# Two grouped-query decode attentions on one core: one cache's K and V loaded in 16 KB runs instead of 8 KB

## The chip, the cores and the metric

The kernel runs on one core of a Trainium2 chip. The time is the device time of one execution in microseconds (us). The profile's span is something else: it runs from the first to the last instruction that the profile records, and here it is about 1.5 us shorter than the time. The experiments were timed in three calls on three chips, so each is compared with the runs of before in its own call.

In the profile PE is the tensor engine's matmuls, PEld its weight loads, DVE the vector engine, ACT the scalar engine, POOL the general engine, and SP the engine that issues the DMAs.

## The reference, cut to what matters

The program computes two independent attention steps for a single new token, A and B, and puts their results side by side. A attends only to the last 2,048 tokens of its cache, B to all 8,192.

```python
# both: x (1,1,576), 32 query heads, 16 KV heads, head size 128, caches (1,16,8192,128), bf16
def attend(x, k_cache, v_cache, wq, wo):
    q = (x @ wq).reshape(1, 1, 32, 128)          # every KV head serves 2 query heads
    k, v = k_cache, v_cache                      # A: the last W = 2048 tokens only
    p = softmax(q @ k.T * 128 ** -0.5)
    return (p @ v).reshape(1, 1, 4096) @ wo      # (1, 1, 576)
out = concatenate([attend(A), attend(B)], axis=-1)
```

Almost no arithmetic is done on each byte that is read. A has 16 MB of K and V, B has 64 MB, the four weight matrices have 18 MB (MB and KB are binary in this paragraph and for packet sizes).

## The kernel before

K and V pass through four 32 KB-per-partition slots in on-chip memory: two for K (`s` = 0, 1), two side by side for V. A run below is a stretch of contiguous bytes that is copied as one; the trace shows one DMA packet for each (2,048 packets of 8 KB for A). The work is cut into five groups of 16 MB: group 0 is all of A, groups 1 to 4 are four heads of B each. The PE program is a loop over the groups; the other engines' programs are unrolled. All large loads go out on SP's queue (the two small x on ACT's), in the order wq of A, wq of B, then K, K, V of each group, then both wo.

```python
def load_k(g, s):                       # 4 MB into slot s
    if g:                               # B: 2 heads, 128 tokens = 32 KB a run
        i = 4 * (g - 1) + 2 * s
        return sp.dma_start(dst, ks[1][0, i:i + 2, :, :].rearrange("e (p t) d -> p e (t d)", t=128))
    for m in range(4):                  # A: 4 DMAs of 2 heads, 32 tokens = 8 KB a run
        i = 4 * m + 2 * s
        src = ks[0][0, i:i + 2, SK - W_A:, :].rearrange("e (p t) d -> p e (t d)", t=32)
        ins = sp.dma_start(dst[:, m * UNIT:(m + 1) * UNIT], src)
        ...                             # cut: semaphore bookkeeping

def load_v(g):                          # 8 MB into both V slots
    if g:                               # B: 4 heads, 256 tokens = 64 KB a run
        return sp.dma_start(dst, vs[1][0, 4 * g - 4:4 * g, :, :].rearrange("h (p t) d -> p h (t d)", t=256))
    for i in range(8):                  # A: 8 DMAs, again 8 KB a run
        m, c = divmod(i, 2)
        src = vs[0][0, 4 * m:4 * m + 4, SK - W_A:, :].rearrange("h (p c t) d -> p h c (t d)", c=2, t=32)[:, :, c, :]
        ...
```

The K tiles are transposed on PE and evicted by ACT and DVE in turn (`L501`, `L504`), then scores, softmax and V sums follow:

```python
if q % 2 == 0: act.activation(kt[:, u % NKT, q * 1024:(q + 1) * 1024], ktps_bf[q], ACT.Copy)   # L501
else:          dve.tensor_copy(kt[:, u % NKT, q * 1024:(q + 1) * 1024], ktps_bf[q])            # L504

def v_sums(g, place):                   # 64 matmuls in the PE loop, the same for every group, L572
    for c in range(2):
        for tt in range(8):
            for j in range(4):
                pe.matmul(opsum[32 * j:32 * j + 32, :], lhsT=ptm[...], rhs=v[:, c, :, b:b + 128], ...)
```

POOL zeroes tiles and makes masks by `affine_select` at the start, later copies slices of q.

```python
for t in (ident, xpad, selq, warm, identf, same, pick, qst): pool.memset(t[:], 0.0)
...
for dj in range(-3, 4): pool.affine_select(same ...)     # 7 selects, L379
for j in range(4):      pool.affine_select(pick ...)     # 4 selects, L379
```

## Time and profile before

| | before |
|---|---|
| time, median of 3 runs | 246.94 us (246.59 to 247.2) |
| profiled run: time / span | 246.54 / 245.0 us |
| data read | 102.8 MB |
| busy: PE / ACT / DVE | 66% / 37% / 34% |

The page of the kernel before, parts 1 to 3, cut. Part 2's rows are 40 equal slices of the span; DMA is the busy share of the 16 DMA engines in tenths:

```profile
span 245.0 us, 5228 instructions
PE 160.8 (66%) x2325; PEld 117.3 (48%) x2325; DVE 82.3 (34%) x145; ACT 91.1 (37%) x95; POOL 10.7 (4%) x48
...
DMA  9999999999999999899999999999989999989993
...
q1 hardware_dynamic: 5052, 102.77, 98.2%
```

No compute engine is near full, and the data queue's packets fill 98.2% of the engines' time. The same in stretches (window, length, busy time and instruction count of PE, PEld, DVE, ACT and POOL, granted PE clock, DMA share, GB/s):

```profile
26.00:56.00 30.00, 22.00 (x336) 17.68 (x324) 12.61 (x23) 15.90 (x17) 0.32 (x2) 0.83 1.01 422
104.00:143.00 39.00, 28.37 (x400) 20.78 (x400) 15.00 (x22) 17.67 (x18) 0.63 (x4) 0.85 1.00 430
143.00:182.00 39.00, 29.09 (x400) 20.75 (x400) 15.01 (x22) 17.58 (x18) 0.63 (x4) 0.81 1.00 432
```

The first line is A's K and V, the others are groups of B. Both are full, but A moves fewer bytes per microsecond. With the DMA engines at a share of 1.00 to 1.01 in these stretches, what is left to change there is the cost of a byte.

Groups by line inside A's stage (30 to 66 us): busy us and mean ns of one, then idle time ahead:

```profile
L501 ACT ACTIVATE kt<-ktps 128x1024 bf16<-128x1024 bf16 x16 | 15.7, 1021 | 13.2 <-PE ktps L495 13.2
L504 DVE COPY kt<-ktps 128x1024 bf16<-128x1024 bf16 x16 | 11.1, 692 | 15.4 <-PE ktps L495 15.4
```

The timeline: POOL's two series of selects, A's V sums, and the issue of B's first V, which A's V sums release:

```profile
3.64 2.91 POOL L379 TENSOR_SCALAR_AFFINE_SELECT same<-same 128x128 f32<-128x128 f32 x7
...
6.75 2.97 POOL L379 TENSOR_SCALAR_AFFINE_SELECT pick<-pick 128x512 f32<-128x512 f32 x4
...
65.88 5.82 PE L572 MATMUL opsum<-slots,ptm 128*32 128x512 bf16 x64 [3.54 <-PEq L214]
...
71.75 0.55 SPq L422 DMA_DIRECT2D slots<-in_B_v_cache_dram  x1
```

The end of the chain that ended last (start, us, what):

```profile
229.58 0.33 SPq L398
229.90 0.04 issue
229.95 12.34 DMA slots<-in_B_wo_dram
242.29 0.04 issue
242.33 0.64 PE ktps L665 x16
242.97 0.02 issue
242.99 0.31 DVE outsb L673
```

The last thing that arrives is a piece of B's wo; 0.64 us of matmuls, a copy, the store of the output and the closing barrier follow.

### The profile page before, as it was taken

The page shows a single profiled execution, that of the slowest core. Times are in us where ns is not written, and L with a number is a line of the kernel's source. Part 1 is how long each engine was busy: PE and PEld are TensorE (multiplying, and loading weights), DVE is VectorE, ACT ScalarE, POOL GpSimd, SP SyncE. Part 2 cuts the span into 40 slices and gives each one's busy share as a digit, 9 for nine tenths or more (in the row PEclk, how much of TensorE's full clock was granted, in tenths as well). Part 3 has the DMA queues.
Part 4 walks back from the last instruction along what each step waited for, and adds up shares of the span by engine and source line. Part 5 has one row for each costly group of instructions (what it writes and reads, how often), then busy time and mean ns, then how long its engine had stood idle before and what let it go on. Part 6 is the DMA issues. An engine that isn't in the chain of part 4 may idle for free. (4 is left out here: it accounts for less than half of the span.)

```text
span 245.0 us, 5228 instructions
## 1 busy us (share of the span) xinstructions
PE 160.8 (66%) x2325; PEld 117.3 (48%) x2325; DVE 82.3 (34%) x145; ACT 91.1 (37%) x95; POOL 10.7 (4%) x48
## 2 busy tenths in 40 slices
PE   0006329994476999383999454999456699647654
PEld 0002129782226876233887221987232678337533
DVE  0001304653222465303556312455322455442300
ACT  2000006875003786301778300687600568620000
POOL 7400000000000000000000000000000000000000
PEclk9999857999575999768899857799857999995999
DMA  9999999999999999899999999999989999989993
GB/s 337 434 434 391 424 427 415 420 423 420 464 428 428 508 397 449 375 428 428 481 419 449 401 407 433 439 492 407 471 375 428 439 482 417 449 386 409 432 402 153
DMA packets 5222, 102.89 MB, mean 420 GB/s; under 512 B 731, under 2 KB 861, under 8 KB 1117
## 3 DMA queue, kind: packets, MB, share of 16 engines
q1 hardware_dynamic: 5052, 102.77, 98.2%
q8 instruction: 6, 0.10, 0.2%
q10 hardware_dynamic: 160, 0.00, 0.0%
q14 instruction: 4, 0.02, 0.0%
HBM read 102.76 MB, written 0.00 MB: 419 GB/s over the span
## 5 line engine op out<-in xcount | busy, mean ns | idle before, releaser
L501 ACT ACTIVATE kt<-ktps 128x1024 bf16<-128x1024 bf16 x80 | 77.9, 1021 | 90.1 <-PE ktps L495 90.1
L495 PE MATMUL ktps<-ident,slots 128*128 128x128 bf16 x1280 | 85.0, 230 | 23.0 <-PEq L214 23.0
L495 PEld LDWEIGHTS ktps<-ident,slots 128*128 128x128 bf16 x1280 | 79.1, 104 | 38.3 <-issue 38.3
L504 DVE COPY kt<-ktps 128x1024 bf16<-128x1024 bf16 x80 | 55.3, 692 | 62.0 <-PE ktps L495 62.0
L572 PE MATMUL opsum<-slots,ptm 128*32 128x512 bf16 x320 | 28.2, 528 | 10.6 <-PEq L214 10.6
L516 PE MATMUL sacc<-kt,qst 128*32 128x512 bf16 x320 | 25.4, 392 | 1.9 <-PEq L214 1.9
L572 PEld LDWEIGHTS opsum<-slots,ptm 128*32 128x32 bf16 x320 | 13.7, 127 | 23.7 <-issue 21.7
L551 PE MATMUL misc<-ident,psb 128*128 128x128 bf16 x40 | 4.7, 288 | 15.8 <-PEq L214 15.8
L538 ACT ACTIVATE psb<-sacc,stat 128x2048 bf16<-128x2048 f32 x5 | 9.8, 1967 | 9.5 <-DVE stat L531 9.5
L583 DVE TENSOR_TENSOR vtmp<-opsum,maskV 128x512 f32<-128x512 f32 x4 | 2.8, 692 | 30.9 <-PE opsum L572 30.9
L551 PEld LDWEIGHTS misc<-ident,psb 128*128 128x128 bf16 x40 | 3.6, 128 | 18.2 <-issue 18.2
L438 PE MATMUL misc<-xnine,twice 64*128 64x18 bf16 x1 | 0.2, 170 | 18.0 <-DMA xnine<-in_B_x_dram 18.0
L485 POOL COPY qst<-qcol 128x8 bf16<-128x8 bf16 x20 | 3.1, 191 | 161.9 <-PE sacc L516 147.5
L665 PE MATMUL ktps<-slots,opj 128*32 128x144 bf16 (+1 forms) x192 | 6.8, 247 | 4.4 <-DMA slots<-in_B_wo_dram 4.4
L558 DVE TENSOR_TENSOR ptm<-misc,maskP 128x1024 bf16<-128x1024 bf16 x5 | 3.5, 692 | 16.0 <-PE misc L551 16.0
L516 PEld LDWEIGHTS sacc<-kt,qst 128*32 128x32 bf16 x320 | 5.0, 94 | 8.0 <-issue 4.3
L438 PEld LDWEIGHTS misc<-xnine,twice 64*128 64x128 bf16 x1 | 0.1, 98 | 18.0 <-issue 18.0
L665 PEld LDWEIGHTS ktps<-slots,opj 128*32 128x32 bf16 x192 | 5.2, 97 | 5.9 <-DMA slots<-in_B_wo_dram 5.3
L462 ACT ACTIVATE qrow<-opsum 128x512 bf16<-128x512 f32 x1 | 0.6, 597 | 19.4 <-PE opsum L456 19.4
L447 DVE TENSOR_SCALAR xpad<-misc,par 128x5 bf16<-128x5 f32 (+1 forms) x8 | 1.2, 230 | 14.2 <-PE misc L438 14.2
L529 DVE TENSOR_REDUCE stat<-sacc 128x1 f32<-128x512 f32 x5 | 3.5, 692 | 4.5 <-PE sacc L516 4.5
L551 PE MATMUL turned<-ident,psb 128*128 128x128 bf16 x40 | 4.8, 293 | 0.0
(73 smaller groups left out, 52.5 us busy)
## 6 DMA issues: line engine op xcount, KB each, us to landing
slots<-in_B_k_cache_dram SPq DMA_DIRECT2D x8, 4096.0 KB
slots<-in_A_k_cache_dram SPq DMA_DIRECT2D x8, 1024.0 KB
slots<-in_A_v_cache_dram SPq DMA_DIRECT2D x8, 1024.0 KB
slots<-in_A_wq_dram SPq DMA_DIRECT2D x1, 4608.0 KB, 13.8
slots<-in_B_wq_dram SPq DMA_DIRECT2D x1, 4608.0 KB, 23.9
slots<-in_A_wo_dram SPq DMA_DIRECT2D x1, 4608.0 KB, 20.8
slots<-in_B_wo_dram SPq DMA_DIRECT2D x1, 3024.0 KB, 27.6
slots<-in_B_wo_dram SPq DMA_DIRECT2D x1, 1008.0 KB, 11.7
```

Of the source, the lines that this page charges most:

```text
L485: ins = pool.tensor_copy(dst, src)
L495: ins = pe.matmul(ktps_bf[q][:, t * 128:(t + 1) * 128], lhsT=slots[:, o:o + 128], rhs=ident[:, :], start=True, stop=True, is_transpose=True)
L501: add("act", lambda act, q=q, dst=dst: act.activation(dst, ktps_bf[q], ACT.Copy), reads=[("bank", q)], writes=[("kt", u % NKT, q)], tag="e ...
L504: add("dve", lambda dve, q=q, dst=dst: dve.tensor_copy(dst, ktps_bf[q]), reads=[("bank", q)], writes=[("kt", u % NKT, q)], tag="e%d%d" % ( ...
L516: ins = pe.matmul(sacc[32 * j:32 * j + 32, :], lhsT=qst[:, o:o + 32], rhs=rhs, start=(u == 0 and e == 0), stop=True, skip_group_check=True)
L529: add("dve", lambda dve: dve.tensor_reduce(st(C_M + g), sacc[:, :], AX.X, ALU.max), reads=[B_S], writes=[("st", C_M + g)], tag="max")
L538: return act.activation(dst, src, ACT.Exp, bias=st(C_NB + g), scale=SCALE, accum_out=st(C_L + g))
L551: ins = pe.matmul(dst[:, t * 128:(t + 1) * 128], lhsT=psb[:, o:o + 128], rhs=ident[:, :], start=True, stop=True, is_transpose=True)
L558: return dve.tensor_tensor(ptm[:, c * 1024:(c + 1) * 1024].rearrange("p (t y) -> p t y", t=8), dst.rearrange("p (t y) -> p t y", t=8), mas ...
L572: ins = pe.matmul(opsum[32 * j:32 * j + 32, :], lhsT=ptm[:, o:o + 32], rhs=v[:, c, :, b:b + 128], start=(c == 0 and tt == 0), stop=(c == 1 ...
L583: add("dve", lambda dve: dve.tensor_tensor(vtmp[:, :, :], src, by, ALU.mult), reads=[B_O, w], writes=["vtmp"], tag="keep")
L665: ins = pe.matmul(ktps[P][32 * j:32 * j + 32, 0:w], lhsT=opj[:, P, jj:jj + 32], rhs=slots[:, o:o + w], start=(jj == 0), stop=(jj == HQ - 1))
```

## The change

The intent is to read A's K and V in runs twice as long, so in half as many packets: 64 tokens (16 KB) per partition instead of 32. That moves tokens within the tiles. K evictions of A sort them back while they write, in runs of two elements. In the V slots the head half `x` and the token half `c` change places for A, so only the matmuls with `c` equal to `x` are shared by A and B; the others stand in two blocks, one run for A and one for B. The masks are made by DVE from one mask instead of by POOL's selects.

```diff
 def load_k(g, s):   # group 0
-    for m in range(4):
-        i = 4 * m + 2 * s
-        src = ks[0][0, i:i + 2, SK - W_A:, :].rearrange("e (p t) d -> p e (t d)", t=32)
-        ins = sp.dma_start(dst[:, m * UNIT:(m + 1) * UNIT], src)
+    for m1 in range(2):
+        i = 8 * m1 + s
+        src = ks[0][0, i:i + 7:2, SK - W_A:, :].rearrange("h (p t) d -> p h (t d)", t=64)
+        ins = sp.dma_start(dst[:, m1 * 2 * UNIT:(m1 + 1) * 2 * UNIT], src)
 def load_v(g):      # group 0
-    for i in range(8):
-        m, c = divmod(i, 2)
-        src = vs[0][0, 4 * m:4 * m + 4, SK - W_A:, :].rearrange("h (p c t) d -> p h c (t d)", c=2, t=32)[:, :, c, :]
+    for i in range(4):
+        m1, x = divmod(i, 2)
+        src = vs[0][0, 4 * i:4 * i + 4, SK - W_A:, :].rearrange("h (p t) d -> p h (t d)", t=64)
 # K evictions
+    if g == 0:
+        dst = bass.AP(tensor=kt, offset=..., ap=[[NKT * UNIT, 128], [2, 256], [1024, 2], [1, 2]])
+        src = src.rearrange("d (y x e) -> d y x e", x=2, e=2)
 # V sums, in the PE loop
-    (one block of 64 matmuls)
+    part(20, None, 0, False)             # c == x: 32 matmuls, every group
+    if g: part(20.2, REST, 1, False)     # c != x: 32 matmuls, groups of B
+    else: part(20.1, FIRST, 1, True)     # c != x, places swapped: 32 matmuls, group 0
 # POOL
-    for dj in range(-3, 4): select(same ...)
-    for j in range(4): select(pick ...)  # DVE makes these masks now
+    (q_stage: four small copies a call instead of two)
 # cut: B's K pairs heads i and i+2, offsets of q and K tiles, DVE's mask making, the order in which A's exp writes, reductions at the end
```

More of the change, by code (lines that the diff above doesn't have):

```diff
@@ L314, in bass_concat_heads__sliding_block_cached__gqa_block_cached__decode_kernel @@
     pickB = nc.alloc_sbuf_tensor("pickB", [128, 4, 32], F32)
-    same = nc.alloc_sbuf_tensor("same", [128, 128], F32)
+    kindA = nc.alloc_sbuf_tensor("kindA", [128, 32], F32)
+    sameA = nc.alloc_sbuf_tensor("sameA", [128, 128], F32)
     sameB = nc.alloc_sbuf_tensor("sameB", [128, 128], F32)
@@ L318, in bass_concat_heads__sliding_block_cached__gqa_block_cached__decode_kernel @@
     onesf = nc.alloc_sbuf_tensor("onesf", [128, 4], F32)
-    qst = nc.alloc_sbuf_tensor("qst", [128, 2 * 264], BF16)
+    qst = nc.alloc_sbuf_tensor("qst", [128, 1024], BF16)
     qcol = nc.alloc_sbuf_tensor("qcol", [128, 2, HQ], BF16)
@@ L369, in setup @@
     def setup(pool):
-        for t in (ident, xpad, selq, warm, identf, same, pick, qst):
+        for t in (ident, xpad, selq, warm, identf, pick, pickB, qst):
             pool.memset(t[:], 0.0)
@@ L373, in setup @@
         return pool.memset(opj[:], 0.0)
-    add("pool", setup, writes=["ident", ("xpad", 0), ("xpad", 1), "selq", "ones", "warm", "identf", "pick", "same",
+    add("pool", setup, writes=["ident", ("xpad", 0), ("xpad", 1), "selq", "ones", "warm", "identf", "pick", "pickB",
                                ("qst", 0), ("qst", 1), ("opj", 0), ("opj", 1)])
@@ L383, in bass_concat_heads__sliding_block_cached__gqa_block_cached__decode_kernel, with sums @@
     add("pool", select(selq[:], 0, [[-32, 4], [-1, 2]], 1), reads=["selq"], writes=["selq"])
-    for dj in range(-3, 4):
-        add("pool", select(same[:], 32 * dj, [[-1, 128]], 1), reads=["same"], writes=["same"])
     add("pool", select(identf[:], 0, [[-1, 128]], 1), reads=["identf"], writes=["identf"])
-    for j in range(4):
-        add("pool", select(pick[:], -128 * j, [[1, 4], [-1, 128]], 4), reads=["pick"], writes=["pick"])
-    def sums(out, view, reads, writes, tag=None):
-        add("dve", lambda dve: dve.tensor_reduce(out, view, AX.X, ALU.add), reads=reads, writes=writes, tag=tag)
+    def sums(out, view, reads, writes, tag=None, axes=AX.X):
+        add("dve", lambda dve: dve.tensor_reduce(out, view, axes, ALU.add), reads=reads, writes=writes, tag=tag)
     sums(par2[:, :], ident[:, :].rearrange("p (m g) -> p g m", g=2), ["ident"], ["par2"])
@@ L405, in go @@
             if g:
-                i = 4 * (g - 1) + 2 * s
-                return sp.dma_start(dst, ks[1][0, i:i + 2, :, :].rearrange("e (p t) d -> p e (t d)", t=128))
-            for m in range(4):
-                i = 4 * m + 2 * s
-                src = ks[0][0, i:i + 2, SK - W_A:, :].rearrange("e (p t) d -> p e (t d)", t=32)
-                ins = sp.dma_start(dst[:, m * UNIT:(m + 1) * UNIT], src)
-                if m < 3:
-                    op.also.append((16, ins))
+                i = 4 * (g - 1) + s
+                return sp.dma_start(dst, ks[1][0, i:i + 3:2, :, :].rearrange("e (p t) d -> p e (t d)", t=128))
+            for m1 in range(2):
+                i = 8 * m1 + s
+                src = ks[0][0, i:i + 7:2, SK - W_A:, :].rearrange("h (p t) d -> p h (t d)", t=64)
+                ins = sp.dma_start(dst[:, m1 * 2 * UNIT:(m1 + 1) * 2 * UNIT], src)
+                if m1 == 0:
+                    op.also.append((32, ins))
             return ins
@@ L422, in go @@
                 return sp.dma_start(dst, vs[1][0, 4 * g - 4:4 * g, :, :].rearrange("h (p t) d -> p h (t d)", t=256))
-            for i in range(8):
-                m, c = divmod(i, 2)
-                src = vs[0][0, 4 * m:4 * m + 4, SK - W_A:, :].rearrange("h (p c t) d -> p h c (t d)", c=2, t=32)[:, :, c, :]
-                o = (4 * c + m) * UNIT
-                ins = sp.dma_start(dst[:, o:o + UNIT], src)
-                if i < 7:
-                    op.also.append((16, ins))
+            for i in range(4):
+                m1, x = divmod(i, 2)
+                src = vs[0][0, 4 * i:4 * i + 4, SK - W_A:, :].rearrange("h (p t) d -> p h (t d)", t=64)
+                o = (2 * x + m1) * 2 * UNIT
+                ins = sp.dma_start(dst[:, o:o + 2 * UNIT], src)
+                if i < 3:
+                    op.also.append((32, ins))
             return ins
@@ L477, in q_stage @@
     def q_stage(g, s):
-        P = min(g, 1)
         def go(pool):
             for e in range(2):
-                dst = bass.AP(tensor=qst, offset=s * 264 + e * 130 + 4 * s, ap=[[528, 128], [40, 4], [1, 2]])
-                o = 4 * s + 2 * e + (8 * (g - 1) if P else 0)
-                src = bass.AP(tensor=qcol, offset=P * HQ + o, ap=[[2 * HQ, 128], [0 if P else 8, 4], [1, 2]])
-                ins = pool.tensor_copy(dst, src)
+                for x in range(2):
+                    o = s * 514 + e * 260 + x * 128
+                    if g:
+                        dst = bass.AP(tensor=qst, offset=o, ap=[[1024, 128], [40, 4], [1, 2]])
+                        src = bass.AP(tensor=qcol, offset=HQ + 8 * (g - 1) + 4 * e + 2 * s, ap=[[2 * HQ, 128], [0, 4], [1, 2]])
+                    else:
+                        dst = bass.AP(tensor=qst, offset=o, ap=[[1024, 128], [80, 2], [40, 2], [1, 2]])
+                        src = bass.AP(tensor=qcol, offset=8 * x + 4 * e + 2 * s, ap=[[2 * HQ, 128], [16, 2], [0, 2], [1, 2]])
+                    ins = pool.tensor_copy(dst, src)
             return ins
-        add("pool", go, reads=[("qcol", P)], writes=[("qst", s)], tag="q%d" % s)
+        add("pool", go, reads=[("qcol", min(g, 1))], writes=[("qst", s)], tag="q%d" % s)
     def k_transpose(g, u, place):
@@ L493, in tr @@
                 for t in range(8):
-                    o = koff(s) + (32 * m + 8 * q + t) * 128
+                    o = koff(s) + (64 * (m // 2) + 32 * (q % 2) + 16 * (m % 2) + 8 * (q // 2) + t) * 128
                     ins = pe.matmul(ktps_bf[q][:, t * 128:(t + 1) * 128], lhsT=slots[:, o:o + 128],
@@ L498, in k_transpose @@
             add("pe", tr, reads=KS[s] + ["ident"], writes=[("bank", q)], loop=(g, place + q / 8, None))
-            dst = kt[:, u % NKT, q * 1024:(q + 1) * 1024]
+            dst, src = kt[:, u % NKT, q * 1024:(q + 1) * 1024], ktps_bf[q]
+            if g == 0:
+                dst = bass.AP(tensor=kt, offset=u % NKT * UNIT + q // 2 * 2048 + q % 2 * 512,
+                              ap=[[NKT * UNIT, 128], [2, 256], [1024, 2], [1, 2]])
+                src = src.rearrange("d (y x e) -> d y x e", x=2, e=2)
             if q % 2 == 0:
-                add("act", lambda act, q=q, dst=dst: act.activation(dst, ktps_bf[q], ACT.Copy),
+                add("act", lambda act, src=src, dst=dst: act.activation(dst, src, ACT.Copy),
                     reads=[("bank", q)], writes=[("kt", u % NKT, q)], tag="e%d%d" % (u, q))
             else:
-                add("dve", lambda dve, q=q, dst=dst: dve.tensor_copy(dst, ktps_bf[q]),
+                add("dve", lambda dve, src=src, dst=dst: dve.tensor_copy(dst, src),
                     reads=[("bank", q)], writes=[("kt", u % NKT, q)], tag="e%d%d" % (u, q))
@@ L514, in mm @@
                     rhs = kt[:, u % NKT, j * 1024:(j + 1) * 1024].rearrange("d (x g) -> d x g", g=2)[:, :, e]
-                    o = s * 264 + e * 128 + m * 32
+                    o = s * 512 + e * 256 + j % 2 * 128 + m * 32
                     ins = pe.matmul(sacc[32 * j:32 * j + 32, :], lhsT=qst[:, o:o + 32], rhs=rhs,
@@ L535, in go @@
         def go(act):
-            src = bass.AP(tensor=sacc, offset=0, ap=[[512, 128], [2, 256], [1, 2], [0, 4]])
-            dst = bass.AP(tensor=psb, offset=0, ap=[[2048, 128], [4, 256], [1024, 2], [1, 4]])
+            if g:
+                src = bass.AP(tensor=sacc, offset=0, ap=[[512, 128], [2, 256], [1, 2], [0, 4]])
+                dst = bass.AP(tensor=psb, offset=0, ap=[[2048, 128], [4, 256], [1024, 2], [1, 4]])
+            else:
+                src = bass.AP(tensor=sacc, offset=0, ap=[[512, 128], [1, 512], [0, 4]])
+                dst = psb[:, :].rearrange("p (y h) -> p y h", h=4)
             return act.activation(dst, src, ACT.Exp, bias=st(C_NB + g), scale=SCALE, accum_out=st(C_L + g))
@@ L560, in softmax_transpose, with v_sums, part, mm @@
         add("dve", put, reads=[res, "maskP"], writes=[("ptm", c)], tag="put%d" % c)
-    def v_sums(g, place):
-        v = slots[:, VOFF:VOFF + 2 * SLOT].rearrange("p (c m y) -> p c m y", c=2, m=4)
-        def mm(pe):
-            for c in range(2):
-                for tt in range(8):
-                    for j in range(4):
-                        o = c * 1024 + tt * 128 + 32 * j
-                        b = (8 * j + tt) * 128
-                        ins = pe.matmul(opsum[32 * j:32 * j + 32, :], lhsT=ptm[:, o:o + 32], rhs=v[:, c, :, b:b + 128],
-                                        start=(c == 0 and tt == 0), stop=(c == 1 and tt == 7), skip_group_check=True)
-            return ins
-        add("pe", mm, reads=[("ptm", 0), ("ptm", 1)] + VS, writes=[B_O], loop=(g, place, None))
+    FIRST = lambda g: g < 1
+    REST = lambda g: g > 0
+    LAST = lambda g: g == NG - 1
+    def v_sums(g):
+        v = slots[:, VOFF:VOFF + 2 * SLOT].rearrange("p (c m x n y) -> p c x m n y", c=2, m=2, x=2, n=2)
+        def part(place, cond, differ, swap):
+            def mm(pe):
+                for tt in range(8):
+                    for j in range(2):
+                        for c in range(2):
+                            x = c ^ differ
+                            o = c * 1024 + tt * 128 + 64 * j + 32 * x
+                            b = (j * 8 + tt) * 128
+                            at = (x, c) if swap else (c, x)
+                            ins = pe.matmul(opsum[64 * j + 32 * x:64 * j + 32 * x + 32, :], lhsT=ptm[:, o:o + 32],
+                                            rhs=v[:, at[0], at[1], :, :, b:b + 128], start=(not differ and tt == 0),
+                                            stop=(differ == 1 and tt == 7), skip_group_check=True)
+                return ins
+            add("pe", mm, reads=[("ptm", 0), ("ptm", 1)] + VS, writes=[B_O], loop=(g, place, cond))
+        part(20, None, 0, False)
+        if g:
+            part(20.2, REST, 1, False)
+        else:
+            part(20.1, FIRST, 1, True)
     def v_keep(g):
@@ L586, in v_keep @@
              [("accs" if last else "acc", g)], "keep")
-    LAST = lambda g: g == NG - 1
     def weights_top(g):
@@ L597, in top @@
         def top(dve):
-            dve.tensor_reduce(srow[0:1, 0, 0:32], wsum[0:1, 0:128].rearrange("p (j h) -> p h j", j=4), AX.X, ALU.max)
+            dve.tensor_reduce(srow[0:1, 0, 0:32].rearrange("p (b y) -> p b y", b=4),
+                              wsum[0:1, 0:128].rearrange("p (a b c y) -> p b y a c", a=2, b=4, c=2), AX.XY, ALU.max)
             return dve.tensor_reduce(srow[0:4, 1, 0:8], wsum[0:4, 128:256].rearrange("p (a r) -> p r a", r=8),
@@ L603, in rep @@
         def rep(dve):
-            src = bass.AP(tensor=srow, offset=0, ap=[[320, 1], [0, 4], [1, 32]])
-            dve.tensor_scalar(srow[0:1, 0, 32:160].rearrange("p (j h) -> p j h", j=4), src, -SCALE, None, ALU.mult)
+            src = bass.AP(tensor=srow, offset=0, ap=[[320, 1], [8, 4], [0, 2], [1, 8]])
+            for a in range(2):
+                to = srow[0:1, 0, 32 + 64 * a:96 + 64 * a].rearrange("p (b c y) -> p b c y", b=4, c=2)
+                dve.tensor_scalar(to, src, -SCALE, None, ALU.mult)
             src = bass.AP(tensor=srow, offset=160, ap=[[320, 4], [0, 16], [1, 8]])
@@ L624, in total @@
         def total(pe):
-            pe.matmul(wsum[:, 264:265], lhsT=same[:, :], rhs=st(C_T + 5), start=True, stop=True)
+            pe.matmul(wsum[:, 264:265], lhsT=sameA[:, :], rhs=st(C_T + 5), start=True, stop=True)
             return pe.matmul(wsum[:, 265:269], lhsT=sameB[:, :], rhs=st(C_T + 6, 4), start=True, stop=True)
-        add("pe", total, reads=[("st", C_T + 5), "same", "sameB"], writes=[B_W], loop=(g, 19.2, LAST))
+        add("pe", total, reads=[("st", C_T + 5), "sameA", "sameB"], writes=[B_W], loop=(g, 19.2, LAST))
         add("dve", lambda dve: dve.reciprocal(st(C_T + 10, NG), wsum[:, 264:269]),
@@ L690, in bass_concat_heads__sliding_block_cached__gqa_block_cached__decode_kernel, with pick_A @@
         q_finish(P)
-    sums(maskV[:, :], same[:, 0:32].rearrange("p (m y) -> p m y", m=4), ["same"], ["maskV"])
+    sums(kindA[:, :].rearrange("p (b y) -> p b y", b=4), identf[:, :].rearrange("p (a b c y) -> p b y a c", a=2, b=4, c=2),
+         ["identf"], ["kindA"], axes=AX.XY)
+    add("dve", lambda dve: dve.tensor_copy(sameA[:, :].rearrange("p (a b c y) -> p a b c y", a=2, b=4, c=2),
+                                           bass.AP(tensor=kindA, offset=0, ap=[[32, 128], [0, 2], [8, 4], [0, 2], [1, 8]])),
+        reads=["kindA"], writes=["sameA"])
+    sums(sameB[:, 0:8], identf[:, :].rearrange("p (x y) -> p y x", y=8), ["identf"], ["sameB0"])
+    add("dve", lambda dve: dve.tensor_copy(sameB[:, 8:128].rearrange("p (a y) -> p a y", y=8),
+                                           bass.AP(tensor=sameB, offset=0, ap=[[128, 128], [0, 15], [1, 8]])),
+        reads=["sameB0"], writes=["sameB"])
+    sums(maskV[:, :], identf[:, :].rearrange("p (j m y) -> p m j y", j=4, m=4), ["identf"], ["maskV"], axes=AX.XY)
+    def pick_A(dve):
+        for r in range(4):
+            dst = bass.AP(tensor=pick, offset=129 * r, ap=[[512, 128], [64, 2], [32, 2], [4, 8]])
+            src = bass.AP(tensor=kindA, offset=0, ap=[[32, 128], [8, 2], [16, 2], [1, 8]])
+            ins = dve.tensor_copy(dst, src)
+        return ins
+    add("dve", pick_A, reads=["kindA", "pick"], writes=["pick"])
+    add("dve", lambda dve: dve.tensor_copy(bass.AP(tensor=pickB, offset=0, ap=[[128, 128], [33, 4], [4, 8]]),
+                                           bass.AP(tensor=sameB, offset=0, ap=[[128, 128], [0, 4], [1, 8]])),
+        reads=["sameB0", "pickB"], writes=["pickB"])
     sums(four[:, :], ident[:, :].rearrange("p (x h) -> p h x", h=4), ["ident"], ["four"])
@@ L695, in bass_concat_heads__sliding_block_cached__gqa_block_cached__decode_kernel @@
         reads=["four"], writes=["maskP"])
-    sums(sameB[:, 0:8], same[:, 0:32].rearrange("p (m y) -> p y m", m=4), ["same"], ["sameB0"])
-    add("dve", lambda dve: dve.tensor_copy(sameB[:, 8:128].rearrange("p (a y) -> p a y", y=8),
-                                           bass.AP(tensor=sameB, offset=0, ap=[[128, 128], [0, 15], [1, 8]])),
-        reads=["sameB0"], writes=["sameB"])
-    sums(pickB[:, :, :], pick[:, :, :].rearrange("p r (i c) -> p r c i", i=4), ["pick"], ["pickB"])
     for g in range(NG):
@@ L723, in bass_concat_heads__sliding_block_cached__gqa_block_cached__decode_kernel @@
             o_columns(0)
-        v_sums(g, 20)
+        v_sums(g)
         v_keep(g)
```

## The prediction

> **What bounds the kernel now.** The DMA engines. The page counts 102.8 MB at a mean of 420 GB/s over a span of 245.0 us and the queue table gives data packets 98.2% of 16 engines' time. PE is busy 66%, ACT 37%, DVE 34%. By stretches, A's K and V (26 to 56 us) move at 420 to 424 GB/s, B's (64 to 184 us) at 432 to 433, both at a DMA share of 1.00 to 1.02: no queue runs dry, only the cost of a byte counts. [...]
>
> **What a packet costs** (the trace's packet records, means): 8 KB 313.8 ns (2,048, A's K and V); 32 KB 1,217.5 ns (B's K); 64 KB 2,423.6 ns (B's V). The last two lie on 37.7 ns per KB plus 11.4 ns a packet, which makes 312.9 ns of 8 KB: that fixed part explains A's lower rate. [...]
>
> **What the change does.**
> 1. A's K and V in 1,024 packets of 16 KB. Estimate from the line: 614 ns each. A's transfers shrink from 2,048 x 313.8 / 16 = 40.2 us to 1,024 x 614 / 16 = 39.3 us: 0.75 to 0.85 us, all on the critical path.
> 2. 8 DMAs, so 128 semaphore packets of 9.3 ns fewer: 0.07 us.
> 3. POOL loses 11 selects (5.9 us), DVE gains small setup operations (about 1 us). They end at 10 and 30 us, the first K lands at 35: nothing.
> 4. A's K evictions are written in runs of two elements. ACT's 1,021 ns should stay; DVE's 692 ns stays, or becomes about 1.2 us [...] (estimate: half the rate). At worst 4 us more in A's K stage. PE waits 3.5 us before A's V sums, which wait for V at 65.8 us; B's first V is issued at 71.8 us and wanted by the queue only at 85. Hidden.
> 5. V sums: 64 matmuls a group as before, half of them behind a condition: perhaps 1 or 2 us of PE per group. In the last group they end at 229.6 us and release the last 1.6 MB of B's wo, but the engines have queued work until about 238. Hidden.
> 6. 20 more POOL copies of q, 191 ns each: hidden.
>
> **Predicted time.** 246.94 - 0.8 = 246.1 us; 80% range 245.3 to 246.9. Faster by over 2%: 1%; within 2%: 97%; slower by over 2%: 2%.
>
> **What would show each step right.** 1,024 packets of 16 KB at 610 to 620 ns. A at about 427 GB/s. A's V sums start at 65.0 instead of 65.9 us, and all later work keeps that lead. B's groups unchanged, about 38.8 us each. No hole in the DMA row, whatever DVE's eviction takes.
>
> **What would make it wrong.** 16 KB runs interleaved over four heads could be read from HBM at another rate. The conditional block or slower evictions could delay a buffer's release beyond its slack of 8 to 14 us: a hole in the DMA row at 85 or 238 us. And the gain is close to the spread of the runs before (246.59 to 247.2), so two medians may not show it.

The 0.8 us are steps 1 and 2 (0.75 to 0.85 and 0.07 us), worked out from the packet records. The 1.2 us of step 4 is an estimate: a one-column instruction of DVE took 154 ns (`L531`), and 154 plus twice the other 538 ns of an eviction makes 1,230; that the rate might halve was the author's guess. The 4 us of step 4 and the 1 or 2 us of step 5 are estimates too, and so is the 85 us: in the trace of before the first packet of B's first V starts at 82.5 us.

## The result, and the profile after

| | before | after |
|---|---|---|
| median, 6 runs each | 246.61 us (246.51 to 247.2) | 246.39 us (246.29 to 246.48) |
| ratio, 95% interval | | 0.9986 (0.9973 to 0.9999) |
| profiled run: time / span | 246.54 / 245.0 us | 246.43 / 244.6 us |

A ratio is the mean time of one kernel's fast runs over that of the other's of the same rounds, so it is not quite the ratio of the medians. A ratio of 0.9986 is about 0.35 us here (0.0014 x 246.7). The kernel seems to have become faster, by less than half of the 0.8 us that the prediction gave: this interval just leaves out 1, that of a second timing (after2 below) does not.

The page after:

```profile
span 244.6 us, 5235 instructions
PE 163.9 (67%) x2325; PEld 119.5 (49%) x2325; DVE 88.2 (36%) x152; ACT 92.5 (38%) x95; POOL 9.1 (4%) x57
...
DMA  8999999999999999899999999998989999989993
...
q1 hardware_dynamic: 3900, 102.76, 98.1%
```

The queue has 1,152 packets fewer: 1,024 of data and 128 of semaphores. It is as full as before. By stretches:

```profile
26.00:56.00 30.00, 19.31 (x276) 15.76 (x269) 15.72 (x26) 14.38 (x14) 0.56 (x4) 0.83 1.00 427
104.00:143.00 39.00, 26.52 (x400) 18.67 (x401) 14.92 (x22) 17.46 (x18) 1.12 (x8) 0.89 1.01 435
143.00:182.00 39.00, 28.45 (x404) 20.89 (x408) 15.01 (x22) 17.67 (x18) 1.12 (x8) 0.85 1.01 434
```

A's stage rose from 422 to 427 GB/s, as predicted. (B's rates differ by a few GB/s because a fixed window cuts packets of 64 KB, which last 2.42 us each; the table of stages below is exact.) The evictions of A's K:

```profile
L507 ACT ACTIVATE kt<-ktps 128x1024 bf16<-128x1024 bf16 x16 | 17.0, 1098 | 16.5 <-PE ktps L497 16.5
L510 DVE COPY kt<-ktps 128x1024 bf16<-128x1024 bf16 x16 | 16.6, 1076 | 15.0 <-PE ktps L497 14.9
```

DVE took 1,076 ns instead of 692, near the 1.2 us that the prediction allowed for; ACT's 1,021 ns became 1,098. The timeline of A's stage:

```profile
55.91 0.73 PE L497 MATMUL ktps<-ident,slots 128*128 128x128 bf16 x10 [3.28 <-issue]
...
68.45 6.51 PE L589 MATMUL opsum<-slots,ptm 128*32 128x512 bf16 x64 [0.87 <-PEq L214]
...
75.01 0.55 SPq L422 DMA_DIRECT2D slots<-in_B_v_cache_dram  x1
```

A's V sums start at 68.45 us, not at 65.0: PE came late, not V, whose last packet ended at 64.67. PE stood still for 3.28 us in the middle of a transpose; a 16 KB instruction packet was read at 53.3 us, within that pause. The pause is at the same PE instruction in two more runs of the change's program (2.67 us in after2, 2.99 in pad8). In compute8, with the same slow evictions, it is 0.38 us, and PE is done with A's scores at 57.5 us, against 57.3 before and 62.6 here: so the slow evictions alone delay PE little. Whether the packet makes the pause, no run tests. The end of the chain:

```profile
235.49 5.12 PE ktps L691 x138
240.61 0.72 issue
241.33 1.22 PE ktps L691 x46
242.55 0.02 issue
242.57 0.31 DVE outsb L699
```

The chain no longer names the DMA, but the last piece of wo still decides: it landed at 241.75 us, 0.48 us earlier than before (242.23), and the last matmul ended 0.77 us after it (0.71 before).

**Where the time went, stage by stage.** A fixed window is too coarse for 0.6 us. From the trace's records of data packets one can add up the bytes moved (each packet's bytes spread evenly over its record) and read when the sum passes the end of each stage. In us:

```
kernel     wq ends   A's 16 MB  B group 1  group 2  group 3  group 4   last data landed
before       23.88       39.97      38.94    38.82    38.78    38.78             242.23
after        23.95       39.33      38.95    38.82    38.78    38.78             241.75
```

The difference lies in A's stage: 0.64 us. All kernels below with 16 KB runs of the change's shape give 39.26 to 39.38, and the two with 8 KB runs 39.84 and 39.97, so it is 0.5 to 0.7 us. (A's stage and B's group 1 together, which does away with packets that straddle the border, take 78.27 to 78.32 us in the seven traces with the change's loads and 78.87 and 78.91 with the old ones: 0.55 to 0.64 us.) B's groups agree to 0.01 us. So PE's lateness in A's stage cost no DMA time at all.

But the time fell by about 0.35, not 0.6. Subtracting span from time, run by run, shows where the rest is: 1.85 us on average for the six runs after (1.79 to 1.91), against 1.50 for 9 runs of before (1.42 to 1.58). They were run at other times. Something takes 0.35 us longer outside the span. The trace has records of POOL's last two instructions (semaphore instructions, which the views leave out). They close the kernel for all engines: the first gathers the arrivals of the other engines, the second releases them.

```
             POOL gathers   POOL releases   apart     SP's last wait ends   time - release seen by PE
before            244.456         244.539    83 ns               244.998                      1.90 us
after             244.036         244.475   439 ns               244.621                      1.85 us
```

These two instructions follow one another without a wait between them, and after the change they stand 0.36 us further apart. The span does not show it, because the span ends with SP's wait for the stored output, which is over later still; the time does, since it ends 1.8 to 1.95 us after PE sees the release in every kernel here. And the trace has an 8 KB packet of instructions at 245.16 us after the change, where before has none (it has one at 28.0 us instead).

### The profile page after: what moved, and what is told of

It reads as the page before. It is cut to its first block, busy times and chain, and to the rows that moved or that the text cites. A ratio compares the mean times of both kernels' runs of the same rounds, so it can differ in the third digit from the quotient of the medians.

```text
span 244.6 us, 5235 instructions
## 1 busy us (share of the span) xinstructions
PE 163.9 (67%) x2325; PEld 119.5 (49%) x2325; DVE 88.2 (36%) x152; ACT 92.5 (38%) x95; POOL 9.1 (4%) x57
## 5 line engine op out<-in xcount | busy, mean ns | idle before, releaser
L507 ACT ACTIVATE kt<-ktps 128x1024 bf16<-128x1024 bf16 x80 | 79.3, 1037 | 90.0 <-PE ktps L497 89.9
L497 PE MATMUL ktps<-ident,slots 128*128 128x128 bf16 x1280 | 86.5, 232 | 22.6 <-PEq L214 19.1
L497 PEld LDWEIGHTS ktps<-ident,slots 128*128 128x128 bf16 x1280 | 80.3, 105 | 38.2 <-issue 38.2
L510 DVE COPY kt<-ktps 128x1024 bf16<-128x1024 bf16 x80 | 60.8, 768 | 57.7 <-PE ktps L497 57.6
L589 PE MATMUL opsum<-slots,ptm 128*32 128x512 bf16 x320 | 29.0, 539 | 11.4 <-PEq L214 11.4
L487 POOL COPY qst<-qcol 128x8 bf16<-128x8 bf16 x40 | 5.5, 191 | 165.0 <-PE sacc L522 145.2
```

The costliest lines, as they stand in the source:

```text
L487: ins = pool.tensor_copy(dst, src)
L497: ins = pe.matmul(ktps_bf[q][:, t * 128:(t + 1) * 128], lhsT=slots[:, o:o + 128], rhs=ident[:, :], start=True, stop=True, is_transpose=True)
L507: add("act", lambda act, src=src, dst=dst: act.activation(dst, src, ACT.Copy), reads=[("bank", q)], writes=[("kt", u % NKT, q)], tag="e%d% ...
L510: add("dve", lambda dve, src=src, dst=dst: dve.tensor_copy(dst, src), reads=[("bank", q)], writes=[("kt", u % NKT, q)], tag="e%d%d" % (u, q))
L589: ins = pe.matmul(opsum[64 * j + 32 * x:64 * j + 32 * x + 32, :], lhsT=ptm[:, o:o + 32], rhs=v[:, at[0], at[1], :, :, b:b + 128], start=(n ...
```

## The experiments

Theories at the start: (1) the fixed cost of a packet is right, but the change's new computing gives half of the gain back somewhere on the critical path; (2) the computing is hidden, and the loads are simply worth less. Once the closing pair was seen, a third came up: (C) the length of POOL's program alone sets the closing pair apart. Kernels that reorder data without the matching computation give a wrong A on purpose; this is said with each.

### dma16: the loads alone

```diff
 # kernel before, group 0 only: load_k and load_v as in the change (t=64, 4 DMAs each); nothing else; A wrong
```

> The kernel before with the change's loads of A's K and V alone (16 KB runs, 4 DMAs each); A's result is wrong on purpose, every other instruction is that of before. Theory 1 (a fixed cost of about 11 ns a packet, all on the critical path, and the change's new compute gives half of the gain back somewhere): 0.8 us below before, so about 0.45 us below the changed kernel. Theory 2 (the new compute is hidden; the loads themselves save only what the changed kernel showed): 0.35 to 0.5 us below before, the same as the changed kernel.

Measured: 245.98 us against 246.79, ratio 0.9980 (0.9966 to 0.9993), some 0.5 us; two of the five runs were at 246.5 and 246.6. A's stage took 39.38 us. This lies between the two expectations and by itself decided nothing. What it does show: the loads alone make A's stage exactly as short as the whole change does.

### compute8: the computing alone

```diff
 # changed kernel, group 0 only: load_k and load_v as before (t=32, 8 DMAs each); nothing else; A wrong
```

> The changed kernel with the old loads of A's K and V (8 KB runs, 8 DMAs each); A's result is wrong on purpose. Theory 1 (new compute gives part back): 0.3 to 0.5 us above before. Theory 2 (new compute hidden): within 0.1 us of before, although DVE's evictions of A take about 1.05 us instead of 0.69 and PE runs 2 to 4 us later.

Measured: 246.97 us, ratio 1.0010 (0.9997 to 1.0024), about 0.25 us above before, an interval that just includes no difference. The span mean is 245.18 us against 245.29 of before, so inside the span the new computing costs nothing; time minus span is 1.86 against 1.50. Theory 1 was right that something is lost and theory 2 that the computing is hidden; neither had the place.

### dma4: runs of half the old length

```diff
 # kernel before, group 0: the same number of DMAs, each partition filled by two 4 KB runs; A wrong
-rearrange("e (p t) d -> p e (t d)", t=32)
+rearrange("e (p t) d -> p e (t d)", t=16)   # dst split into two halves per partition; V likewise
```

> The kernel before with A's K and V in 4,096 runs of 4 KB, in as many DMAs as before (8 and 8); A's result is wrong on purpose. A fixed cost per packet of 11.4 ns (from the line through 32 and 64 KB) gives 2,048 x 11.4 / 16 = 1.46 us more than before, packets of about 162 ns. If runs of another size were only worth half of that at the end of the kernel, as the changed kernel suggests: about 0.7 us more.

Measured: 247.77 us, ratio 1.0040 (1.0027 to 1.0054), about 1.0 us above before, between the two expectations. Packets of 4 KB took 163.3 ns, as the line gives. A's stretch:

```profile
26.00:56.00 30.00, 22.80 (x344) 17.50 (x336) 12.60 (x23) 15.79 (x17) 0.31 (x2) 0.89 1.03 409
```

Note the share, 1.03: a share above 1 means that the records of packets overlap. The packets' own time rose by 1.67 us an engine (41.80 against 40.13), but the stage only by 1.16 (41.13 against 39.97). So a packet's record has a fixed part of 11 to 13 ns (11.4 by the line, 13.1 from 4 to 8 KB), of which the overlap of the records hides some. What the stage pays is (41.13 - 39.97) x 16 / 2,048 = 9.1 ns a packet. That is why 0.8 us was too much for the change.

### dmabig: long runs, first try

```diff
 # kernel before, group 0: one DMA a K slot and one for V; A wrong
+ks[0][0, s:s + 15:2, SK - W_A:, :].rearrange("h (p t) d -> p h (t d)", t=128)   # 16 runs of 32 KB of each of 8 heads
+vs[0][0, :,          SK - W_A:, :].rearrange("h (p t) d -> p h (t d)", t=256)   # 8 runs of 64 KB of each of 16 heads
```

> The kernel before with A's K in 256 runs of 32 KB (one DMA a slot) and V in 128 runs of 64 KB (one DMA), as B's groups are loaded; A's result is wrong on purpose. Fixed cost per packet: (2,048 - 384) x 11.4 / 16 = 1.19 us less, and 13 DMAs fewer, 0.12 us: 1.2 to 1.3 us below before. If only half of it reaches the end: about 0.6 us below.

Measured: 342.69 us, ratio 1.39, a miss by 97 us, in the wrong direction. During the loads of A's K and of A's V:

```profile
26.00:56.00 30.00, 14.03 (x174) 10.20 (x170) 6.67 (x14) 7.47 (x8) 0.00 (x0) 0.66 1.00 212
140.00:160.00 20.00, 0.00 (x0) 0.00 (x0) 0.00 (x0) 0.00 (x0) 0.00 (x0) 0.50 0.44 97
```

K moves at half the usual rate with all engines busy; V, with 8 runs of each head, keeps less than half of the engines busy as well. The queue carried 350 semaphore packets, 8 fewer than in big2 with as many DMAs, where a DMA has 16: so V's load went out on 8 engines, it seems. Run length was not the only thing that this edit changed. Two runs take it apart.

### big2: long runs spread as B's are

```diff
 # kernel before, group 0: B's access patterns on whole heads of A's caches (same bytes, wrong tokens); A wrong
+ks[0][0, 2 * s:2 * s + 2, :, :].rearrange("e (p t) d -> p e (t d)", t=128)   # 64 runs of each of 2 heads
+vs[0][0, 0:4, :, :].rearrange("h (p t) d -> p h (t d)", t=256)               # 32 runs of each of 4 heads
```

> The kernel before with A's K in 256 runs of 32 KB and V in 128 of 64 KB, read and spread over the partitions as B's groups are (64 or 32 runs of each head side by side; whole heads of A's caches instead of the last 2,048 tokens, so A's result is wrong on purpose, and the bytes are the same). If the run length alone counts: 1.0 to 1.3 us below before. If such long runs are slow for A's caches for a reason of the memory: far above before, as the first try with long runs was (342.7 us).

Measured: 245.88 us, ratio 0.9968 (0.9954 to 0.9983), about 0.8 us below before (1.0 to 1.3 were expected), and A's stage 39.04 us, 0.93 less. Long runs of A's caches are not slow. The packets' own time fell by 1.23 us an engine (38.90 against 40.13), so the stage again follows by three quarters, as with 4 KB (1.16 of 1.67) and 16 KB (about 0.6 of 0.77).

### p16: the change's packets, spread over 16 runs of a head

```diff
 # kernel before, group 0: 16 KB runs, 4 DMAs each, but 8 heads x 16 runs instead of 4 heads x 32; A wrong
+rearrange("h (p t) d -> p h (t d)", t=64)   # of 8 heads and half of the tokens
```

> The changed kernel's packets (16 KB, 4 DMAs each) on the kernel before, but each DMA takes 16 runs of each of 8 heads instead of 32 runs of each of 4; A's result is wrong on purpose. Theory P (the first try with long runs was slow because 16 runs of a head [...]): A's 39 us of loads become some 80, so about 285 us in all, packets of 16 KB at 1.0 to 1.3 us instead of 0.61. Theory L (it was slow because of its long runs): within 0.5 us of the loads of the changed kernel, 246 us.

Measured, one run: 282.9 us, and A's stretch at half speed:

```profile
26.00:56.00 30.00, 14.10 (x180) 11.09 (x172) 6.87 (x14) 7.86 (x9) 0.00 (x0) 0.60 1.00 221
```

The packets are the change's, 16 KB each, but their median is 1,207 ns instead of 612. So theory P holds as far as the shape goes: 16 runs of each head in a DMA halve the rate (221 GB/s in this window), 32 (427 in dma16) or 64 (big2's K, its whole stage 39.04 us) do not. Why is not shown: no trace here tells which engine wrote which partition, and no run tried eight heads side by side, 2 or 4 MB apart in the caches, with more runs of each. For the change this means that its step to 16 KB, with 32 runs of each head, was the longest of the run lengths tried in this pattern that kept the full rate; the next doubling leaves 16 runs.

### after2: the changed kernel again

> The changed kernel itself, unedited, five more rounds beside the others of this call. Theory 1 (its new compute costs 0.2 to 0.3 us): 0.3 to 0.4 us below before, as when it was first timed. Theory 2 (hidden compute, the first timing was chance): 0.55 to 0.7 us below before, as the loads alone.

The kernel is unedited. Measured: 246.66 us against 246.67, ratio 0.9993 (0.9979 to 1.0008), about 0.2 us below before by the means, which is neither expectation. A's stage 39.36 us, closing pair 435 ns apart, time minus span 1.84 us. Five runs fell in two clumps, 246.25 and 246.7, and the spans differ by the same 0.5 us (244.4 and 244.9). The clumps appear in other kernels too (dma16, pad8). The traces show where the time goes. From the end of B's group 4 to the last landing, the stage of the wo loads, three traces took 23.47 to 23.56 us (after2, dma16b and pad8, each the slowest of its five runs); the others of this length took 23.06 to 23.24. In these three the last DMA engine ended 1.42 to 1.50 us after the mean of the 16, in the others 1.0 to 1.24 (read from the last 128 packets, followed from one to the next). Why one engine falls behind stays open. One run of before took 384.61 us and is counted nowhere.

### lean: the change without its two suspected computing costs

```diff
 # changed kernel; A wrong
-    if g == 0: dst = ..., src = ...              # evictions of A as of B
-    part(20, None, ...); part(20.1, FIRST, ...); part(20.2, REST, ...)
+    one block of the same 64 matmuls, no condition
```

> The changed kernel without the two suspected computing costs: A's evictions are written as B's are (DVE keeps 0.69 us instead of 1.05), and the V matmuls stand in one block without a condition; A's result is wrong on purpose. Theory 1 (these cost something on the critical path): 0.2 to 0.3 us below the changed kernel, 0.6 below before. Theory 2 (hidden): the same as the changed kernel within 0.1 us. In both, A's V sums should start when V lands (about 65 us) instead of at 68.5.

Measured: 246.34 us, ratio 0.9988 (0.9974 to 1.0002). Groups in A's stage, and A's V sums:

```profile
L503 ACT ACTIVATE kt<-ktps 128x1024 bf16<-128x1024 bf16 x16 | 15.7, 1021 | 13.2 <-PE ktps L497 13.2
L506 DVE COPY kt<-ktps 128x1024 bf16<-128x1024 bf16 x16 | 11.1, 692 | 15.2 <-PE ktps L497 15.2
```

```profile
65.53 1.47 PE L584 MATMUL opsum<-slots,ptm 128*32 128x512 bf16 x12 [3.33 <-PEq L214]
```

The evictions are fast again and the V sums start when V lands, 2.9 us earlier, and the time hardly follows. The times alone do not decide it: lean is 0.3 us below before, and the changed kernel (after2) lies 0.15 us above lean by the means and 0.32 by the medians, with intervals that overlap widely. The traces do: A's stage took 39.34 us against 39.33 and 39.36, the last data landed at 241.83 us, between the 241.75 and 241.99 of the two traces of the changed kernel, and the last matmul ended 0.76 to 0.77 us after it in all three. So neither the evictions nor the conditional block shows a cost. The closing pair is still 435 ns apart, and time minus span 1.84 us.

### pad8: eight tiny POOL instructions more

```diff
 # changed kernel, POOL's setup; the result stays right
+    spare = nc.alloc_sbuf_tensor("spare", [128, 8], F32)
+    for i in range(8):
+        pool.memset(spare[:, i:i + 1], 0.0)
     pool.memset(onesf[:], 1.0)
```

> The changed kernel plus eight one-column memsets in POOL's setup, nothing else; the result stays right. In the traces so far POOL's last two instructions, which close the kernel for all engines, stand 435 to 439 ns apart in the four kernels with the change's program and 83 to 84 ns in the five with the old one, and an 8 KB instruction packet follows there about 0.7 us later. Theory C (POOL's program [...], by its length alone): [...] the gap is 83 ns, the time outside the span falls from 1.85 to 1.5 us, and the kernel is 0.5 to 0.65 us below before (about 246.1), 0.3 to 0.35 below the changed kernel. Theory W (the change's work itself delays the end): the gap stays, 0.2 to 0.35 us below before as the changed kernel.

What theory C says is that the length of POOL's program alone decides, and that eight instructions more close the gap.

Measured: correct, 246.13 us against 246.72, ratio 0.9971 (0.9958 to 0.9985), about 0.7 us below before. The closing pair is 84 ns apart, and time minus span is 1.43 us in all five runs (1.42 to 1.44). This is theory C: with more instructions than the changed kernel, it is further below before than that kernel was in either timing (0.35 and 0.17 us). The intervals of the ratios overlap; the closing pair and the time outside the span do not.

### rev: the old program, POOL shortened

```diff
 # dma16, POOL's setup; wrong on purpose (two masks all ones)
-    11 selects of same and pick
+    20 one-column memsets of a spare tile
```

> The kernel before with the loads of the change alone, as tried, with POOL's program cut to the change's length: 11 selects taken out, 20 one-column memsets put in; the result is wrong on purpose (two masks are all ones). Everything after the setup is as before. Theory C: the gap between POOL's last two instructions becomes about 435 ns and the 0.35 us is lost here too: 0.2 to 0.3 us below before instead of 0.6. Theory W: 83 ns, 0.5 to 0.65 us below before.

Measured: 246.4 us, ratio 0.9988 (0.9974 to 1.0001), about 0.3 us below before. The closing pair is 434 ns apart, time minus span 1.84 us. Nothing of the change's computing is in this kernel, and POOL does less work than in dma16; its program only has the change's number of recorded instructions, 69 instead of 71 (pad8 has 77; semaphore instructions are counted). The 0.35 us comes back.

### dma16b: the loads alone, again

> The loads of the change alone on the kernel before, as tried, five more rounds beside the two others: 0.5 to 0.65 us below before under either theory; under theory C the padded changed kernel comes within 0.1 us of it.

The same kernel as dma16, beside pad8 and rev. Measured: 246.16 us, ratio 0.9973 (0.9959 to 0.9986), about 0.65 us below before, and within 0.05 us of pad8 by the means (246.14 and 246.09).

### The closing pair in all kernels

```
kernel      POOL's last two, apart   time - span, mean (runs)   8 KB instruction packet at
before                       83 ns              1.50 us (26)                      28.0 us
dma16                        83 ns              1.53 us (5)                       27.6 us
dma16b                       83 ns              1.50 us (5)                       28.7 us
dma4                         83 ns              1.51 us (5)                       28.0 us
big2                         83 ns              1.52 us (5)                       28.9 us
p16                          84 ns              1.59 us (1)                       31.3 us
dmabig                       84 ns              1.49 us (5)                       31.4 us
pad8                         84 ns              1.43 us (5)                       92.0 us
after                       439 ns              1.85 us (6)                      245.2 us
after2                      435 ns              1.84 us (5)                      245.7 us
lean                        435 ns              1.84 us (5)                      245.3 us
compute8                    435 ns              1.86 us (5)                      245.8 us
rev                         434 ns              1.84 us (5)                      245.2 us
```

The last column is one of the three 8 KB instruction packets that each trace has after its start; the other two lie at 77 to 89 us (p16: 124, dmabig: 181) and 120 to 125 us (p16: 158, dmabig: 218). All kernels fall in one of two groups, and of what was varied only the length of POOL's program sorts them. How the length acts is not shown: in the five kernels with the wide pair the packet comes 0.7 to 1.0 us after the release, so it cannot itself be what POOL waited for.

## Why the prediction was right or wrong

- **The bound was right.** The DMA engines are the bottleneck from start to end, and no difference in A's stage is lost in B's groups: they took 38.95, 38.82, 38.78 and 38.78 us in the changed kernel, and the same within 0.12 us in every other kernel but the two with slow loads. The wo stage after them is less even (23.06 to 23.56 us, see after2).
- **The mechanism was right, its size was not (steps 1 and 2).** 1,024 packets of 16 KB took 614.8 ns on average, median 612, and 128 semaphore packets fell away, as predicted. (The recorded 313.8 ns takes in instruction packets of 8 KB; the data alone took 313.5.) But A's stage became about 0.6 us shorter (0.5 to 0.7), not the 0.8 to 0.9 of steps 1 and 2. The term was worked out from the duration of packet records, as if packets on an engine never overlapped. With 8 KB runs they do a little (40.13 us of the packets' own time an engine in a stage of 39.97), with 4 KB runs more (41.80 in 41.13), with the long runs of big2 not (38.90 in 39.04). The stage pays 7 to 10 ns a packet, by the 4, 8 and 16 KB kernels and without the semaphore packets, not 11.4.
- **Step 3 failed, and with it step 6 as far as the copies lengthen POOL's program.** "They end at 10 and 30 us, the first K lands at 35: nothing." POOL's work was indeed hidden; its program was not. Taking out 11 selects with their waits and putting in 20 copies changed its length, and 0.35 us of the gain was lost in the closing barrier. pad8 takes the loss away and rev makes it anew, so the length as the cause is shown; how it acts is not.
- **Steps 4 and 5, and the work of step 6, were hidden as predicted.** DVE's evictions took 1,076 ns and A's V sums began 2.6 us later than before, not 0.9 earlier as the prediction said; but B's first V was issued at 75.0 us, 7 us or more before the engines reached it (82.1), and lean shows that nothing was lost. The last V sums ended 3.7 us later than before (233.2 against 229.5), and the engines still had queued work (share 0.97 from 234 to 236 us). Hardly any of that lateness is the change's: dma16, with the old computing, ended them at 231.8, pad8, with the new, at 231.0.
- **The sum.** 0.6 us of DMA time gained less 0.35 us lost in the closing barrier makes 0.25; measured were 0.35 and 0.17 in two timings. The predicted 246.1 us came out as 246.39.
- **What was luck.** The number came close because two errors cancel in part: before was taken at 246.94 us, the median of three runs, and stands at 246.61 with six, so the same 0.8 us from there would have given 245.8. And the range of 245.3 to 246.9 holds before's own 246.61: a change without any effect would have fallen in it too.

## What to carry to other kernels

In this kernel, whose data packets fill 98% of the DMA engines' time, a longer run saved some 7 to 10 ns of an engine per packet that disappeared; take such a figure from the lengths of whole stages, since the records of short packets overlap (at 4 KB 41.80 us of records an engine in a stage of 41.13). Before lengthening runs further, measure the pattern: 32 or 64 runs of each head kept the full rate here (427 GB/s in dma16), 16 halved it (221 in p16). When a gain is smaller than the DMA records promise, compare time minus span: what happened in the closing barrier here was in the time and hardly in the span (1.85 us outside it against 1.50). The length of POOL's program was itself a variable: eight idle instructions at its start were worth 0.35 us, over half of what the longer runs gained.
